# A fused transpose-and-gate product taken apart: plain transposes, column quarters and a summing product in a retention and mixture-of-experts kernel

## The chip, the cores and the metric

The kernel runs on one core of a Trainium2 chip. The metric is the time of one execution on the device in microseconds (us). TensorE is called PE (its weight loads PEld), VectorE DVE, ScalarE ACT, GpSimd POOL, and SyncE SP; SP only issues transfers here.

## The reference

Retention over q, k and v (4 batches, 8 heads, 768 tokens, 64 dims) gives x with 3072 tokens of 512 features. x goes through a noisy top-2 gate over 8 experts and two-layer experts.

```python
gamma = 1.0 - 2.0 ** (-5.0 - np.arange(H))
for t in range(S):
    state = gamma[None, :, None, None] * state + np.einsum('bhd,bhe->bhde', k[:, :, t], v[:, :, t])
    y[:, :, t] = scale * np.einsum('bhd,bhde->bhe', q[:, :, t], state)
x = y.transpose(0, 2, 1, 3).reshape(B * S, H * D)
...
logits = x @ w_gate
noisy_logits = logits + np.log1p(np.exp(x @ w_noise)) * noise
top2 = np.argpartition(-noisy_logits, 2, axis=1)[:, :2]
# top2_w: softmax of the two chosen noisy logits
...
out[mask] += top2_w[mask, k, None] * (np.maximum(x[mask] @ w1[e], 0.0) @ w2[e])
```

## The kernel before, in words

The tokens are cut into 24 tiles of 128 (6 chunks for each of 4 batches). One loop over the tiles, j = 0 to 23, computes the retention, writes x as two f16 halves to xbuf in HBM, and makes the gate logits. Behind it the experts run one after another: `mm1` (L858 to L860, three f16 products for each block) and `mm2` (L890 to L892), with rows gathered from xbuf and added into `out` by indirect transfers.

The order of the work on each engine is the order in which the Python code calls it: the schedule is manual, the engines run their own queues in order, and semaphores join them. `todo`, `mid`, `middle` and `first_todo` are tables from a loop index to extra work (expert 0's weights, the routing of earlier tiles); `at` and `P` enter things in them. After the loop `early(n)` issues the next n units of expert 0's `mm1` between routing steps.

One iteration j does, on PE, in this order: `qk(j+1)` (L327, scores of the next tile, two row halves of the array at once), `x_turn(j-1)` (L375 and L379), `y_state(j)` (L342, four quarters of the array), `y_mm(j)` (L349, two column halves) and the state update pU (L358, column halves; not in the last chunk of a batch, and no `y_state` in the first).

`x_turn` is called the turn below. y lies by feature in four groups of 128. Its f32 products take a group as the weights and multiply it by `turn`, a table of 144 columns: the identity (128) beside 16 columns of gate weights. So one product gives the group by token and its part of the 16 logits; the pairs of groups accumulate in PSUM so that two partial logits are left (`lgs`). L379 sums squares of a token over the features with four one-column products.

On DVE, `qk`'s scores are masked (`am`), then `x_scale(j-1)` makes a power-of-two scale from the sum of squares (p2m, xsa), then come the `mid` entries, then `x_split`'s low half (L405). On ACT: `x_split`'s high half (x), `logits(j-1)` (copy of `lgs`), the copies yt and U, the squares sq, and the `first_todo` entries. POOL scales v (vp) and q (qs). `turn_table` fills the two tables on DVE in iterations 0 and 3, once the constants `ct` (with the identity) and the weights `wgf` have landed. `route_x` adds the two partial logits (lg, L416) and applies softplus on ACT.

SP issues the loads of tile j+4, the x writes (L406), expert 0's weights, `x_t` (a transposing transfer of gathered rows) and the seven writes of zeros into `out` (L273, L276), two of them in iterations 22 and 23.

Of the kernel before, what the change touches and what calls it, by code (L numbers as in the profile page):

```python
# [10 lines left out]
F32 = mybir.dt.float32  # L11
# [5 lines left out]
OP = mybir.AluOpType  # L17
# [3 lines left out]
C = 128  # L21
# [24 lines left out]
XW = 128 + 2 * E  # L46
# [7 lines left out]
for _n, _w in (("mask", 128), ("vtab", NC * H), ("gtab", NC * HP), ("ident", 128), ("tri", 128), ("lanes", 128), ("blks", NCOL),  # L54
               ("lidx", NL), ("base", NL), ("rcap", E - 1), ("tie", E - 1), ("tok1", NCH), ("tokv", NCH * 2), ("pad", 1), ("i64", 64)):
    _C[_n] = (_o, _o + _w)
    _o += _w
CW = _o
SOON = _C["gtab"][1]
# [3 lines left out]
def _constants():  # L63
# [6 lines left out]
    put("ident", np.eye(128))  # L70
    put("mask", p[None, :] >= p[:, None])
# [26 lines left out]
def moe_kernel(ctx, tc, qT, kT, kt, vt, noise, wgn, w1, w2, ctab, qtab, xbuf, out):  # L98
# [21 lines left out]
    ct = consts.tile([128, CW - SOON], F32, name="ct")  # L120

    def K(n):
        a, b = _C[n]
        return cs[:, a:b] if b <= SOON else ct[:, a - SOON:b - SOON]

    wgf = consts.tile([128, 2 * KT * 2 * E], F32, name="wgf")
# [25 lines left out]
    turn = consts.tile([128, 2, KT, XW], F32, name="turn")  # L152
# [125 lines left out]
    def turn_table(v):  # L278

        w = wgf.rearrange("p (v k e) -> p v k e", v=2, e=2 * E)[:, v].rearrange("p (s k) e -> p s k e", s=2)  # L280
        t = turn[:, v].rearrange("p (s k) x -> p s k x", s=2)
        for k in range(2):
            nc.vector.tensor_copy(t[:, :, k, k * 2 * E:k * 2 * E + 128], ident[:, None, :].to_broadcast([128, 2, 128]))
            nc.vector.tensor_copy(t[:, :, k, 128 - k * 128:XW - k * 128], w[:, :, k])

# [5 lines left out]
    VP, AM, QS, PY, PT, YT, XS, SQ, LG = {}, {}, {}, {}, {}, {}, {}, {}, {}  # L291
# [24 lines left out]
    nc.scalar.dma_start(ct, ctab[:, SOON:])  # L316
    q_table(2)
    nc.scalar.dma_start(wgf, wgn)
# [26 lines left out]
    def y_mm(j):  # L345
        c = j % NC
        for i in range(HP):
            for s in range(2):
                nc.tensor.matmul(yplace(j, i, s), VP[j][:, 2 * i + s, :], AM[j][:, s, i, :],  # L349
                                 start=(not c and i < 2), stop=True, skip_group_check=True)  # L350
        YT[j] = loads.tile([128, 2, 2, C], F32, name="yt", bufs=2)
        y = YT[j].rearrange("p s g c -> p (s g c)")
        nc.scalar.activation(y.rearrange("p (s x) -> p s x", s=2), PY.pop(j)[:, :, :2 * C], AF.Copy)
        if c < NC - 1:
            for i in range(HP):
                for s in range(2):
                    h = 2 * i + s
                    nc.tensor.matmul(pU[s * 64:s * 64 + 64, i, :], IN["kt", j][:, h * 64:h * 64 + 64], VP[j][:, h, :],  # L358
                                     start=(c == 0 and i == 0), stop=True, skip_group_check=True)
            nc.scalar.activation(U[(c + 1) % 2], pU, AF.Copy)  # L360
        SQ[j] = loads.tile([128, KT, C], BF, name="sq", bufs=1)
        nc.scalar.activation(SQ[j].rearrange("p n c -> p (n c)"), y, AF.Square)

    def x_turn(j):
# [3 lines left out]
        t = loop_psum.tile([128, 2, 512], F32, name="pT").rearrange("p s x -> p (s x)")  # L368
        PT[j] = p = t[:, 512 - 2 * XW:512 + 2 * XW]
        p = p.rearrange("p (s x) -> p s x", s=2)  # L370
        PT[j, "s"] = t[:, 512 + 2 * XW:513 + 2 * XW]
        y = YT.pop(j)
# [7 lines left out]
        PT[j, "y"] = PT[j].rearrange("p (n x) -> p n x", x=XW)[:, :, :128]  # L380

    def logits(j):
        g = min(j // NC, 3) // 2 + j // (3 * NC)
        c0, n = SPAN[g]
        p = PT.pop(j)
        if j == c0:
            LG[g] = temp([128, n, 2 * E], F32, "lg", n)
            LG[g, "s"] = temp([128, n, 2, 2 * E], F32, "lgs", n)
        nc.scalar.activation(LG[g, "s"][:, j - c0], p.rearrange("p (s x) -> p s x", s=2)[:, :, 128:XW], AF.Copy)
# [7 lines left out]
    def x_split(j, between=None):  # L397
        x = work.tile([128, 2, DM], F16, name="x16", bufs=3)
        py = PT.pop((j, "y"))
        xv = [x[:, a].rearrange("p (n x) -> p n x", n=KT) for a in range(2)]  # L400
# [9 lines left out]
    def route_x(g, c0, c1):  # L410
# [4 lines left out]
        ls = LG[g, "s"][:, c0:c1]  # L415
        nc.vector.tensor_tensor(LG[g][:, c0:c1], ls[:, :, 0], ls[:, :, 1], op=OP.add)  # L416
# [352 lines left out]
    at(21, x_t, 0, 1)  # L769
# [10 lines left out]
    at(0, turn_table, 0)  # L780
    at(3, turn_table, 1)
# [20 lines left out]
    for i in range(2):  # L802
        at(22 + i, zero_out, i)
# [147 lines left out]
    early(1)  # L951
# [9 lines left out]
    early(2)  # L961
# [12 lines left out]
    early(1)  # L974
# [216 lines left out]
```

## Time and profile before

| | us |
|---|---|
| median of 3 runs | 670.21 |
| lowest and highest run | 668.01 and 672.22 |
| the profiled execution | 668.68 |
| its span, first to last instruction | 666.8 |

The profiled execution is one execution of the same program, so a row of it stands against 668.68, of which 1.9 us lie outside the span. Times within the span count from its start. A product's start in PE's timeline is when it is issued; its listed length runs to its result and overlaps the next, so the time that a block takes is read from its start to the start of the next block.

### The profile page before, as it was taken

The page shows a single profiled execution, that of the slowest core. Times are in us where ns is not written, and L with a number is a line of the kernel's source. Part 1 is how long each engine was busy: PE and PEld are TensorE (multiplying, and loading weights), DVE is VectorE, ACT ScalarE, POOL GpSimd, SP SyncE. Part 2 cuts the span into 40 slices and gives each one's busy share as a digit, 9 for nine tenths or more (in the row PEclk, how much of TensorE's full clock was granted, in tenths as well). Part 3 has the DMA queues.
Part 4 walks back from the last instruction along what each step waited for, and adds up shares of the span by engine and source line. Part 5 has one row for each costly group of instructions (what it writes and reads, how often), then busy time and mean ns, then how long its engine had stood idle before and what let it go on. Part 6 is the DMA issues. An engine that isn't in the chain of part 4 may idle for free.

```text
span 666.8 us, 12957 instructions
## 1 busy us (share of the span) xinstructions
PE 644.3 (97%) x5305; PEld 398.9 (60%) x5305; DVE 292.3 (44%) x711; ACT 297.2 (45%) x544; POOL 201.6 (30%) x158
## 2 busy tenths in 40 slices
PE   7999999999999999999999999999999999999991
PEld 5998888648678645554555455545554565455540
DVE  4668887799775221622162216221622162214110
ACT  4678665214544443444454445444444354433210
POOL 3555454042243054104330432043204410440111
PEclk9999999999999999999999999999999999999997
DMA  9999988947297456645673567466736672662212
GB/s 325 394 385 389 342 287 225 364 104 252 73 182 228 119 105 127 196 131 98 124 202 129 97 126 203 124 98 124 205 119 106 122 230 83 126 113 31 32 16 34
DMA packets 90861, 112.87 MB, mean 169 GB/s; under 512 B 57232, under 2 KB 57616, under 8 KB 87216
## 3 DMA queue, kind: packets, MB, share of 16 engines
q1 hardware_dynamic: 78736, 84.95, 41.7%
q0 software_dynamic: 11344, 26.22, 21.2%
q8 instruction: 43, 0.70, 0.4%
q10 hardware_dynamic: 720, 0.84, 0.4%
q14 instruction: 18, 0.15, 0.1%
HBM read 72.67 MB, written 26.21 MB: 148 GB/s over the span
## 4 chain that ended last, share of the span: by engine, by line
PE 74%; DVE 4%; DMA 4%; issue 3%; ACT 1%; POOL 1%; POOLq 0%; ACTq 0%
PE pH L858 12%; PE pH L860 11%; PE pH L859 11%; PE pO L892 11%; PE pO L890 11%; PE pO L891 11%; DMA out<-ot,idx 2%; PE pT L375 1%; DMA xe<-xg 1%; PE pY L349 1%; PE pA L327 1%; PE pT L905 1%; PE pT L904 1%; PE pT L903 1%; DVE w2l L227 1%
## 5 line engine op out<-in xcount | busy, mean ns | idle before, releaser
L879 POOL DMA_INDIRECT out<-ot,idx x54 | 90.7, 1680 | 341.6 <-ACT ot L874 217.2
L858 PE MATMUL pH<-xe,w1h 128*128 128x384 f16 (+5 forms) x576 | 180.9, 314 | 0.9 <-DVE hl L862 0.4
L860 PE MATMUL pH<-xe,w1l 128*128 128x384 f16 (+5 forms) x576 | 181.0, 314 | 0.0
L859 PE MATMUL pH<-xe,w1h 128*128 128x384 f16 (+5 forms) x576 | 181.0, 314 | 0.0
L891 PE MATMUL pO<-w2l,hh 128*128 128x512 f16 x384 | 145.6, 379 | 0.4 <-DVE w2l L227 0.4
L892 PE MATMUL pO<-w2h,hl 128*128 128x512 f16 x384 | 145.6, 379 | 0.1
L890 PE MATMUL pO<-w2h,hh 128*128 128x512 f16 x384 | 145.6, 379 | 0.0
L862 DVE SCALAR_TENSOR_TENSOR hl<-pH,hh 128x384 f16<-128x384 f32 (+5 forms) x144 | 75.1, 526 | 144.9 <-ACT hh L861 144.7
L861 ACT ACTIVATE hh<-pH 128x384 f16<-128x384 f32 (+5 forms) x144 | 67.0, 466 | 132.0 <-PE pH L860 117.7
L874 ACT ACTIVATE ot<-pO,gse 128x512 f32<-128x512 f32 (+4 forms) x54 | 37.1, 687 | 171.7 <-PE pO L892 161.2
L220 DVE SCALAR_TENSOR_TENSOR w1l<-wst,wsc,w1h 128x1024 f16<-128x1024 f32 x28 | 35.8, 1284 | 105.2 <-ACT w1h L215 105.2
L724 POOL DMA_INDIRECT xg<-xbuf,idx x54 | 57.1, 1058 | 64.1 <-DVE wacc L632 31.9
L859 PEld LDWEIGHTS <-w1h 128*128 128x128 f16 x576 | 56.3, 98 | 31.0 <-issue 1.4
L860 PEld LDWEIGHTS <-w1l 128*128 128x128 f16 x576 | 56.2, 98 | 31.0
L858 PEld LDWEIGHTS <-w1h 128*128 128x128 f16 x576 | 56.3, 98 | 30.8 <-issue 0.6
L192 ACT ACTIVATE junk<-wst 128x1024 bf16<-128x1024 f32 x64 | 67.2, 1049 | 0.0
L892 PEld LDWEIGHTS <-hl 128*128 128x128 f16 x384 | 37.5, 98 | 46.6 <-issue 1.0
L890 PEld LDWEIGHTS <-hh 128*128 128x128 f16 x384 | 37.5, 98 | 44.8 <-ACT junk L192 0.3
L891 PEld LDWEIGHTS <-hh 128*128 128x128 f16 x384 | 37.5, 98 | 44.0
L299 POOL TENSOR_TENSOR vp<-in_v,cs 128x512 f32<-128x512 f32 x24 | 26.3, 1094 | 47.2 <-issue 26.9
L215 ACT ACTIVATE w2h<-wst,wsc 128x1024 f16<-128x1024 f32 x32 | 36.5, 1140 | 1.4 <-DVE wsc L170 1.4
L215 ACT ACTIVATE w1h<-wst,wsc 128x1024 f16<-128x1024 f32 x32 | 36.1, 1138 | 1.2 <-DVE wsc L170 1.2
(170 smaller groups left out, 651.0 us busy)
## 6 DMA issues: line engine op xcount, KB each, us to landing
wst<-w SPq DMA_DIRECT2D x28, 1024.0 KB, 7.6
in_q<-qT SPq DMA_DIRECT2D x24, 256.0 KB, 5.8
in_k<-kT SPq DMA_DIRECT2D x24, 256.0 KB, 5.7
in_v<-vt SPq DMA_DIRECT2D x24, 256.0 KB, 5.4
in_kt<-kt SPq DMA_DIRECT2D x24, 256.0 KB, 5.2
xbuf<-x SPq DMA_DIRECT2D x24, 256.0 KB, 4.7
out<-zero SPq DMA_DIRECT2D x6, 1024.0 KB, 7.1
wst<-w SPq DMA_DIRECT2D x8, 512.0 KB, 6.0
```

The lines of the kernel that those rows point to most:

```text
L192: nc.scalar.activation(junk, st[:, i * 1024:(i + 1) * 1024], AF.Square, accum_out=ss[:, i:i + 1])
L215: nc.scalar.activation(hi, st[:, i * 1024:(i + 1) * 1024], AF.Copy, scale=sc[:, 0:1])
L724: nc.gpsimd.indirect_dma_start(out=x[:n], out_offset=None, in_=xbuf[:128 + B0 * S] if e == 0 and t < 3 else xbuf, in_offset=bass.IndirectO ...
L858: nc.tensor.matmul(p[:, :n], whi, xh, start=(k == 0), stop=False)
L859: nc.tensor.matmul(p[:, :n], whi, xl, start=False, stop=False)
L860: nc.tensor.matmul(p[:, :n], wlo, xh, start=False, stop=(k == KT - 1))
L861: nc.scalar.activation(hh[:, f, n0:n1], p[:, :n], AF.Relu)
L862: nc.vector.scalar_tensor_tensor(hl[:, f, n0:n1], p[:, :n], 0.0, hh[:, f, n0:n1], op0=OP.max, op1=OP.subtract)
L879: nc.gpsimd.indirect_dma_start(out=out, out_offset=bass.IndirectOffsetOnAxis(ap=idx[:n, i:i + 1], axis=0), in_=ot[:n], in_offset=None, com ...
L890: nc.tensor.matmul(p, a, WT["2h"][:, f, :], start=(f == 0), stop=False)
L891: nc.tensor.matmul(p, a, WT["2l"][:, f, :], start=False, stop=False)
L892: nc.tensor.matmul(p, c, WT["2h"][:, f, :], start=False, stop=(f == FT - 1))
```

## The change

The turn is taken apart. The four groups of y go through plain transposes against the identity into a PSUM bank of their own (pT). The logits are made by feature: four f32 products with the gate weights as the stationary operand, padded to 32 columns, one for each group, each into its own 32 PSUM partitions (a column quarter of the array) of a second bank (pG). ACT copies the quarters to SBUF (gt), and one f32 product with `pick` (`pick(j-1)`, issued in `y_mm(j)` between y_mm's products and the state update) sums them by token. `logits` then copies 16 columns straight to `lg`, so the tables `turn` and the addition in `route_x` go. The identity and `pick` come in a transfer of their own (`ci`), `wgf` is twice as large, and all seven zero writes stand behind the loop. `x_t(0, 1)` moves from `todo` to `mid`.

```diff
 def _constants():
+    put("pick", np.tile(np.eye(32)[:, :2 * E], (4, 1)))
...
-    nc.scalar.dma_start(ct, ctab[:, SOON:])
+    nc.scalar.dma_start(ci, ctab[:, SOON:THEN])
+    nc.scalar.dma_start(wgf.rearrange("p v k e -> p (v k e)"), wgn)
     q_table(2)
-    nc.scalar.dma_start(wgf, wgn)
+    nc.scalar.dma_start(ct, ctab[:, THEN:])
...
         nc.scalar.activation(y.rearrange("p (s x) -> p s x", s=2), PY.pop(j)[:, :, :2 * C], AF.Copy)
+        if j:
+            pick(j - 1)
         if c < NC - 1:
...
             nc.scalar.activation(U[(c + 1) % 2], pU, AF.Copy)
+        if j:
+            logits(j - 1)
         SQ[j] = loads.tile([128, KT, C], BF, name="sq", bufs=1)
...
-        for s in range(2):
-            for g in range(2):
-                nc.tensor.matmul(p[:, s, g * 128:g * 128 + XW], y[:, s, g, :], turn[:, v, 2 * s + g],
-                                 start=(g == 0), stop=True, skip_group_check=True)
+        for n in range(KT):
+            nc.tensor.transpose(p[:, n * C:(n + 1) * C], y[:, n], ident)
+        for n in range(KT):
+            nc.tensor.matmul(t[n * 32:(n + 1) * 32, :C], wgf[:, v, n], y[:, n], start=True, stop=True, skip_group_check=True)
+        PT[j, "s"] = t[:, C:C + 1]
         q = SQ.pop(j)
         for n in range(KT):
             nc.tensor.matmul(PT[j, "s"], q[:, n], oneb[:, 0:1], start=(n == 0), stop=(n == KT - 1), skip_group_check=True)
+        GT[j] = work.tile([128, C], F32, name="gt", bufs=2)
+        nc.scalar.activation(GT[j], t[:, :C], AF.Copy)
+
+    def pick(j):
+        nc.tensor.matmul(PT[j][:, C + 1:C + 1 + 2 * E], GT.pop(j), K("pick"), start=True, stop=True, skip_group_check=True)
...
-        nc.scalar.activation(LG[g, "s"][:, j - c0], p.rearrange("p (s x) -> p s x", s=2)[:, :, 128:XW], AF.Copy)
+        nc.scalar.activation(LG[g][:, j - c0], PT.pop(j)[:, C + 1:C + 1 + 2 * E], AF.Copy)
...
         nc.scalar.activation(xv[0], py, AF.Copy, scale=XS[j])
-        logits(j)
-        if between:
-            between()
...
-        nc.vector.tensor_tensor(LG[g][:, c0:c1], ls[:, :, 0], ls[:, :, 1], op=OP.add)
...
-    at(21, x_t, 0, 1)
+    P(21, x_t, 0, 1)
...
-    at(0, turn_table, 0)
-    at(3, turn_table, 1)
...
-    for i in range(2):
-        at(22 + i, zero_out, i)
...
     early(1)
-    zero_out(2)
+    zero_out(0)
+    zero_out(1)
     x_turn(j)
     x_scale(j)
-    x_split(j, lambda: route_x(2, 0, NC))
+    x_split(j)
+    early(1)
+    pick(j)
+    logits(j)
+    route_x(2, 0, NC)
     route_d(1)
...
-    early(1)
+    zero_out(2)
     zero_out(3)
...
-    early(2)
+    early(3)
...
-    early(1)
     own_c(1)
```

On PE, one iteration of the loop before, from the last sum of squares of one tile to the first of the next:

```order
L379 MATMUL pT<-oneb,sq 128x1
L342 MATMUL pY<-qs,U_160 64x128 x8
L349 MATMUL pY<-am,vp 64x128 x8
L358 MATMUL pU<-vp,in_kt 64x64 x8
L327 MATMUL pA<-qs,in_k 128x128 x8
L375 MATMUL pT<-turn,yt 128x144 x4
L379 LDWEIGHTS sq
```

and the same iteration after:

```order
L377 MATMUL pG<-oneb,sq 128x1
L337 MATMUL pY<-qs,U_160 64x128 x8
L344 MATMUL pY<-am,vp 64x128 x8
L382 MATMUL pG<-ci,gt 128x16
L355 MATMUL pU<-vp,in_kt 64x64 x8
L322 MATMUL pA<-qs,in_k 128x128 x8
L371 MATMUL pT<-ci,yt 128x128 x4
L373 MATMUL pG<-yt,wgf 32x128 x4
L377 LDWEIGHTS sq
```

The summing product (L382) stands between y_mm and pU, and the turn is two blocks (L371, L373) in place of one.

On ACT, where expert 0's first weights are cast (w1h) ahead of the turn's readers, before (with what each instruction waits for):

```order
L362 ACTIVATE sq<-yt 128x512 [waits Activation_49]
L215 ACTIVATE w1h<-wst_391,wsc_393 128x1024 [waits DVE_49]
L215 ACTIVATE w1h<-wst_391,wsc_393 128x1024
L401 ACTIVATE x_1007<-pT,xsa 128x512 [waits DMAHW0_49,DVE_49,PE_49]
L389 ACTIVATE lgs_310<-pT 128x32
L353 ACTIVATE yt<-pY 128x512 [waits PE_49]
```

and after:

```order
L361 ACTIVATE sq<-yt 128x512 [waits Activation_49]
L217 ACTIVATE w1h<-wst_401,wsc_403 128x1024 [waits DVE_49]
L217 ACTIVATE w1h<-wst_401,wsc_403 128x1024
L379 ACTIVATE gt<-pG 128x128 [waits PE_49]
L401 ACTIVATE x_1077<-pT,xsa 128x512 [waits DMAHW1_49,DVE_49]
L348 ACTIVATE yt<-pY 128x512 [waits PE_49]
```

The copy gt comes in ahead of x, behind the casts, and the copy of the logits has left this place.

On DVE, the same place in the loop, x_scale and what stands behind it, before:

```order
L330 TENSOR_TENSOR am<-pA,cs 128x512 [waits PE_49] x2
L394 TENSOR_SCALAR p2m<-pT 128x1 [waits PE_49]
L395 TENSOR_SCALAR xsa<-p2m 128x1 [waits DVE_49]
L227 SCALAR_TENSOR_TENSOR w1l<-wst_391,wsc_393,w1h 128x512 [waits Activation_49]
L227 SCALAR_TENSOR_TENSOR w1l<-wst_391,wsc_393,w1h 128x512
L227 SCALAR_TENSOR_TENSOR w1l<-wst_391,wsc_393,w1h 128x512 [waits Activation_49]
L405 SCALAR_TENSOR_TENSOR x_1007<-pT,xsa,x_1007 128x512 [waits DMAHW0_49,DVE_49,Activation_49]
```

and after:

```order
L325 TENSOR_TENSOR am<-pA,cs 128x512 [waits PE_49] x2
L394 TENSOR_SCALAR p2m<-pG 128x1 [waits Activation_49]
L395 TENSOR_SCALAR xsa<-p2m 128x1 [waits DVE_49]
L229 SCALAR_TENSOR_TENSOR w1l<-wst_401,wsc_403,w1h 128x512 x3
L402 SCALAR_TENSOR_TENSOR x_1077<-pT,xsa,x_1077 128x512 [waits DMAHW1_49,Activation_49]
```

p2m waited for PE and now waits for ACT; the instruction that it waits for is gt.

## Rows read from the trace of the kernel before

**Rows 1.** The page: the span, and part 1, busy time of each engine.

```profile
span 666.8 us, 12957 instructions
PE 644.3 (97%) x5305; PEld 398.9 (60%) x5305; DVE 292.3 (44%) x711; ACT 297.2 (45%) x544; POOL 201.6 (30%) x158
```

**Rows 2.** The table by stretch: us; busy time and count of PE, PEld, DVE, ACT, POOL; PEclk; DMA; GB/s.

```profile
20.00:117.00 97.00, 93.72 (x1556) 84.04 (x1547) 74.21 (x245) 64.47 (x138) 49.43 (x43) 1.00 0.97 336
200.00:640.00 440.00, 439.87 (x2844) 242.30 (x2843) 137.09 (x240) 189.71 (x313) 117.27 (x87) 1.00 0.56 129
```

**Rows 3.** Waits of PE and its weight loads, 0 to 130 us: total, times, longest.

```profile
PEld pT L375 <- ACT sq L362: 3.0, 6, 1.1
PEld pT L375 <- issue: 1.1, 1, 1.1
PEld pT L375 <- ACT yt L353: 0.4, 1, 0.4
PEld pT L375 <- ACT U L360: 0.2, 1, 0.2
PEld pA L327 <- POOL qs L305: 1.3, 1, 1.3
PE pA L327 <- DVE turn L284: 1.2, 1, 1.2
```

**Rows 4.** PE's timeline, turn of tile 20 to 21: start, us, engine, line, tile, array cut.

```profile
102.78 1.16 PE L327 MATMUL pA<-qs,in_k 64*128 64x128 f32 x16
103.87 1.25 PE L375 MATMUL pT<-turn,yt 128*128 128x144 f32 x8
104.96 0.24 PE L379 MATMUL pT<-oneb,sq 128*128 128x1 bf16 x4
105.13 0.67 PE L342 MATMUL pY<-qs,U 64*64 64x128 f32 x16
105.73 1.09 PE L349 MATMUL pY<-am,vp 128*64 128x128 f32 x16
106.65 0.63 PE L358 MATMUL pU<-vp,in_kt 128*64 128x64 f32 x16
107.22 1.16 PE L327 MATMUL pA<-qs,in_k 64*128 64x128 f32 x16
108.31 1.25 PE L375 MATMUL pT<-turn,yt 128*128 128x144 f32 x8
```

**Rows 5.** PE's timeline, four transposes between mm1 products.

```profile
194.20 0.60 PE L914 MATMUL pO<-ct,yt 128*64 128x128 f32 x4
194.64 0.27 PE L858 MATMUL pH<-xe,w1h 128*128 128x256 f16 x1
```

**Rows 6.** The timeline of weight loads where L202 stands between L358 and L327.

```profile
51.62 0.10 PEld L202 LDWEIGHTS <-oneb 128*128 128x128 bf16 x1
51.73 0.64 PEld L327 LDWEIGHTS pA<-qs,in_k 64*128 64x128 f32 x10
```

**Rows 7.** ACT's timeline, a copy of 32 columns and one of 256.

```profile
101.82 0.19 ACT L389 ACTIVATE lgs<-pT 128x32 f32<-128x32 f32 x1
102.94 0.38 ACT L360 ACTIVATE U<-pU 128x256 f32<-128x256 f32 x1
```

**Rows 8.** ACT's timeline, iteration 10.

```profile
53.26 2.19 ACT L215 ACTIVATE w1h<-wst,wsc 128x1024 f16<-128x1024 f32 x2
```

**Rows 9.** DVE's timeline, iteration 10.

```profile
54.40 0.15 DVE L394 TENSOR_SCALAR p2m<-pT 128x1 int32<-128x1 int32 x1
...
56.64 0.74 DVE L405 SCALAR_TENSOR_TENSOR x<-pT,xsa,x 128x512 f16<-128x512 f32 x1
```

**Rows 10.** DVE's timeline, iteration 18: the lg addition.

```profile
94.32 0.44 DVE L416 TENSOR_TENSOR lg<-lgs 128x96 f32<-128x96 f32 x1
```

**Rows 11.** The chain that ended last: start, us, what.

```profile
153.74 10.86 DMA out<-ot,idx
```

**Rows 12.** SP's timeline: two transposes of xg in one row.

```profile
107.71 3.52 SPq L731 DMA_TRANSPOSE xe<-xg  x2
```

More of the change, by code (lines that the diff above doesn't have):

```diff
@@ L53 @@
 _o = 0
-for _n, _w in (("mask", 128), ("vtab", NC * H), ("gtab", NC * HP), ("ident", 128), ("tri", 128), ("lanes", 128), ("blks", NCOL),
+for _n, _w in (("mask", 128), ("vtab", NC * H), ("gtab", NC * HP), ("ident", 128), ("pick", 2 * E), ("tri", 128), ("lanes", 128), ("blks", NCOL),
                ("lidx", NL), ("base", NL), ("rcap", E - 1), ("tie", E - 1), ("tok1", NCH), ("tokv", NCH * 2), ("pad", 1), ("i64", 64)):
@@ L58 @@
 CW = _o
-SOON = _C["gtab"][1]
+SOON, THEN = _C["gtab"][1], _C["pick"][1]
 WARM, BUSY = 10, 4
@@ L119, in moe_kernel @@
     cs = consts.tile([128, SOON], F32, name="cs")
-    ct = consts.tile([128, CW - SOON], F32, name="ct")
+    ci = consts.tile([128, THEN - SOON], F32, name="ci")
+    ct = consts.tile([128, CW - THEN], F32, name="ct")
     def K(n):
         a, b = _C[n]
-        return cs[:, a:b] if b <= SOON else ct[:, a - SOON:b - SOON]
-    wgf = consts.tile([128, 2 * KT * 2 * E], F32, name="wgf")
+        if b <= SOON:
+            return cs[:, a:b]
+        return ci[:, a - SOON:b - SOON] if b <= THEN else ct[:, a - THEN:b - THEN]
+    wgf = consts.tile([128, 2, KT, 32], F32, name="wgf")
     nz = consts.tile([128, NCH, E], F32, name="nz")
@@ L151, in moe_kernel @@
     xsa = consts.tile([128, NCH], F32, name="xsa")
-    turn = consts.tile([128, 2, KT, XW], F32, name="turn")
     pR = psum.tile([128, 512], F32, name="pR")
@@ L276, in zero_out @@
             nc.sync.dma_start(out[:128, :], zero)
[L278 to L284, printed above, removed]
     U = []
@@ L367, in x_turn @@
         v = int(b >= B0)
[L368 to L372, printed above, removed]
-        for s in range(2):
-            for g in range(2):
-                nc.tensor.matmul(p[:, s, g * 128:g * 128 + XW], y[:, s, g, :], turn[:, v, 2 * s + g],
-                                 start=(g == 0), stop=True, skip_group_check=True)
+        PT[j, "y"] = p = loop_psum.tile([128, 512], F32, name="pT")
+        PT[j] = t = loop_psum.tile([128, 512], F32, name="pG")
+        y = YT.pop(j).rearrange("p s g c -> p (s g) c")
+        for n in range(KT):
[3 more added lines that the diff above has]
+        PT[j, "s"] = t[:, C:C + 1]
         q = SQ.pop(j)
@@ L395, in x_scale, with x_split @@
         nc.vector.tensor_scalar(XS[j].bitcast(I32), m[:, :1], -1.0, float((127 + TX + 62) << 23), op0=OP.mult, op1=OP.add)
-    def x_split(j, between=None):
+    def x_split(j):
         x = work.tile([128, 2, DM], F16, name="x16", bufs=3)
         py = PT.pop((j, "y"))
-        xv = [x[:, a].rearrange("p (n x) -> p n x", n=KT) for a in range(2)]
+        xv = [x[:, a] for a in range(2)]
         nc.scalar.activation(xv[0], py, AF.Copy, scale=XS[j])
-        logits(j)
-        if between:
-            between()
         nc.vector.scalar_tensor_tensor(xv[1], py, XS[j], xv[0], op0=OP.mult, op1=OP.subtract)
@@ L807, in moe_kernel @@
     qk(0)
-    t = loop_psum.tile([128, 2, 512], F32, name="pT")
+    t = loop_psum.tile([128, 512], F32, name="pT")
     for i in range(BUSY):
-        nc.tensor.matmul(t[:, 0], warm[:, :128], warm, start=True, stop=True)
+        nc.tensor.matmul(t, warm[:, :128], warm, start=True, stop=True)
     for j in range(NCH):
@@ L1172 @@
     nz[:, B0 * NC:] = nz[:, B0 * NC:][:, :, turn]
-    wg = [np.concatenate([moe_w_gate[:, o], moe_w_noise[:, o]], 1)[PERM].reshape(KT, 128, 2 * E).transpose(1, 0, 2)
+    wg = [np.pad(np.concatenate([moe_w_gate[:, o], moe_w_noise[:, o]], 1)[PERM], ((0, 0), (0, 32 - 2 * E)))
+          .reshape(KT, 128, 32).transpose(1, 0, 2)
           for o in (list(range(E)), turn)]
```

9 lines of the change are left out of this document (2 added, 7 removed).

## The prediction

> **What bounds the kernel now.** I read the page first. TensorE (PE) is busy for 644.3 of 666.8 us [rows 1], so I asked where its idle time lies. The table of stretches says: in the token loop (20 to 117 us) PE is busy for 93.7 of 97 us at a granted clock of 1.00, and from 200 to 640 us for 439.9 of 440 [rows 2]. Nothing behind the loop can soak up a delay, so what the loop gains or loses arrives at the end almost one for one.
>
> Inside the loop I read PE's own timeline from turn to turn (L375 of tile 20 at 103.87 to L375 of tile 21 at 108.31, 4.44 us) [rows 4], and count iterations that way below, by the tile whose turn ends them. PE goes from block to block without idle time, so only the cost of the blocks counts. Last I read what the turn itself, the block that is rewritten, waits for: its weight loads waited 4.7 us in all, in nine of the iterations [rows 3]. The loop has that slack and no more.
>
> **What a change of tile shape costs now.** The blocks of [rows 4] use different cuts of the array: L327 two row halves, L375 and L379 the whole, L342 four quarters, L349 and L358 two column halves. A lone f32 pass of 128 columns takes 0.11 us: the four transposes of L914 take 194.20 to 194.64 [rows 5]. L349 has 16 passes, two abreast: 8 x 0.11 = 0.88 of its 0.92. L342 has 16, four abreast: 4 x 0.11 = 0.44, but lasts 0.60. L327 has 16, two abreast: 0.88, but lasts 1.09. L358, 64 columns wide, should take 8 x 0.055 = 0.44 and lasts 0.57. L349 is followed by a block of its own shape; the other three are followed by another shape and carry 0.16, 0.21 and 0.13 us more than their passes. So a change of shape costs 0.13 to 0.21 us, and the changed loop has more of them.
>
> **The change, part by part.**
>
> *The turn on PE.* Now: L375 with 8 passes of 144 columns, 1.09 us, and L379, 0.17: 1.26 us. Then: four transposes, one pass each (L914 shows one each), 0.44, and a change to column quarters behind them, for which I take 0.20, like L327, which also loads 128 columns of f32: 0.64. Then eight passes of 128 columns for the logits, four abreast, as L342 runs them: 2 x 0.11 + 0.16 = 0.38. Then L379's four, 0.17. Together 1.19 us: only 0.07 less than now. If the changes of shape were free it would be 0.44 + 0.22 + 0.17 = 0.83.
>
> *The product that sums the quarters* stands between L349 and L358, which run today with no change of shape between them. It is f32, whole array, so two passes with two weight loads and 16 columns each, too short to hide a load. The nearest row is L202, one product of 4 columns between L358 and L327, where a change exists anyway: 0.11 us from 51.62 to 51.73 [rows 6]. So the lower bound is 0.11; with a change in (0.16), twice 0.11, and a change out (0.13) it is 0.50. I take 0.50, because both changes are new. In iterations without L358 (5 and 23; the last chunk of a batch keeps no state) one change is there already: 0.34.
>
> PE's iteration thus grows by 0.50 - 0.07 = 0.43 us, by 0.27 in iterations 5 and 23. [...]
>
> *A longer chain from PE to DVE.* x_scale's first step on DVE (p2m) waited for PE's squares; it now waits for ACT's copy gt, as the order shows. gt has 128 columns; the copies of 32 and of 256 take 0.19 and 0.38 us [rows 7], so I take 0.25, and with the extra handover 0.27. The product waits for p2m too, but stands 1.5 us of PE work (L342, L349) behind the turn [rows 4], so that costs nothing by itself. The logits copy moves on ACT from ahead of yt to just ahead of the squares, which PE needs only after the transposes and the quarters, a microsecond into the turn: nothing. Where the turn waits for x_split (iterations 9 to 12, 15, 17 to 19), this lies on the path. Iteration 10 is worse: ACT runs two w1h casts from 53.26 for 2.19 us [rows 8]. p2m ran at 54.40, beside them; gt stands behind them in ACT's queue and ends at about 55.7, so p2m, the three w1l steps queued behind it on DVE, the low half of x (56.64) [rows 9] and the next turn move by 1.3 us. The other seven I put at 0.26 on average: 0.27 for gt or, where PE becomes the later one, 0.43 less the old wait, less the lg addition (0.44 us) [rows 10], which leaves DVE's chain in two of them.
>
> *DVE's turn tables* go. The 1.2 us that PE waited for them ahead of L327 is not won: the same L327 also waited for POOL's qs (1.3 us) [rows 3], which nothing moves. *The small transfers* on ACT's queue are one more, with some 64 KB more of weights; against 0.97 of DMA share in the loop [rows 2] I count nothing, at most half a microsecond either way.
>
> *Zero writes and x_t on SP's queue.* Two writes of 1 MB leave iterations 22 and 23 and are issued behind the loop with the other five; one transpose goes ahead of tile 20's x write. Behind them on SP stand the x writes of the last tiles and, much later, the next weight loads. The scatter into out ran at 153.74 [rows 11], 37 us behind the loop's end, so writes that come some 2 us later are hidden; without that cover it would cost those 2 us. The transposes, issued by 111.2 [rows 12], have a longer loop to land in.
>
> *Behind the loop* the mm1 units change places by one, and as many of them stand ahead of the last routing steps as before. One lg addition leaves DVE's chain (-0.44) and with it a handover from ACT; gt (0.27) comes in, and PE gets the last product between whole-array matmuls, where no shape changes (twice 0.11), beside DVE's chain: -0.3 us, at most 0.3 the other way.
>
> **The sum.** Iterations bound by PE: 12 x 0.43 = 5.2; iterations 5 and 23: 0.5; iteration 22, where PE waits 0.4 for yt [rows 3] and the product fills that wait: 0.15. The eight that wait: 1.3 + 7 x 0.26 = 3.1. Loop +9.0, behind it -0.3: **+8.7 us**. The profiled execution took 668.68 us, so 677.4; the median of the runs is 1.5 higher, 670.21, which makes **679 us**.
>
> **Rivals.**
>
> 1. *The turn gets cheaper, and the kernel is not slower* (chance 0.19). If the added loads and changes of shape overlap with the passes as L202's nearly does, an iteration has 0.44 + 0.22 + 0.17 + 0.11 = 0.94 in place of 1.26. It decides when the 0.74 us that I add for loads and changes is really under 0.32. Fully so, 15 iterations give -4.8, the eight about +1: 666 us. For it: L349's passes show almost no extra. Against it: L342, L327 and L358 each carry theirs, in the same places of every iteration. [...]
>
> 2. *The quarters run one after another* (0.10). Then their eight passes take 0.88, not 0.22: +0.66 in each of 15 iterations, and gt and p2m come later by as much in the eight: about 14 more, 693 us. Against it: L342 has four tiles at once. For it: those differ in rows too, which the four quarters do not.
>
> 3. *The gt chain decides in more iterations* (0.10): with 0.8 in four more places where ACT's queue holds a cast or a sum ahead of gt, +3: 682 us.
>
> 4. *The zero writes meet the weight loads or the scatter* (0.03): 681 us.
>
> 5. *The clock falls* (0.01). [...]
>
> **How the numbers follow.** The forecast has 0.57 and by itself spans 672 to 684: the change of shape between 0.13 and 0.21, the product between 0.2 and 0.6. To 8 in 10 I reach down to 668, which takes in about half of rival 1, and up to 689; rivals 2 and 5 and the rest of rival 1 stay out. A difference under 1% (6.7 us) is about what runs of this kernel can't tell from none. Above 676.9: 0.35 of the forecast and 0.24 of rivals 2 to 5: 0.59. Within: 0.22 of the forecast and 0.15 of rival 1: 0.37. Under 663.5: 0.04, for a rival 1 that gains on DVE's side too.
>
> **What would show it.** In the changed loop's timeline L371 to L373 about 0.64, L373 to L377 about 0.38, L382 to L355 about 0.5 apart, and an undisturbed iteration near 4.87 us; p2m idle before it until gt; the first L858 near 124 us in place of 115, and from there on the same lengths as now. I am wrong if L382 lies within 0.2 us, or if the quarters' eight passes start one behind another.

## The result and the profile after

The changed kernel is slower: a median of 678.6 us (676.24 to 680.84, six runs) against 671.96 us for the kernel before in the same six rounds (668.01 to 673.9), a ratio of 1.0118 with a 95% interval of 1.0088 to 1.0149. The profiled execution took 676.53 us (668.68 before); the sum had said 677.4 for it and 679 for the median.

The page, its span and busy times, and the table by stretch (columns as in [rows 2]):

```profile
span 674.7 us, 13272 instructions
...
PE 652.3 (97%) x5449; PEld 395.2 (59%) x5449; DVE 292.5 (43%) x699; ACT 304.0 (45%) x568; POOL 201.5 (30%) x158
```

```profile
20.00:117.00 97.00, 92.30 (x1551) 74.14 (x1543) 70.35 (x219) 66.89 (x151) 50.15 (x43) 1.00 0.93 322
...
200.00:640.00 440.00, 439.75 (x2887) 245.13 (x2883) 141.97 (x259) 191.67 (x316) 119.64 (x89) 1.00 0.57 132
```

Behind the loop PE is as full as before [rows 2]. The loop ends later, as PE's timelines show, first that of the kernel before:

```profile
115.12 0.34 PE L858 MATMUL pH<-xe,w1h 128*128 128x384 f16 x1
```

```profile
123.65 0.32 PE L849 MATMUL pH<-xe,w1h 128*128 128x384 f16 x1
```

The first mm1 product starts 8.5 us later. In what follows "the loop's end" is the start of that product. From there to the first mm2 product (L890 before, L881 after) it is 17.76 us before and 17.49 after, so 0.27 came back behind the loop. The span grew by 7.9, but what is left of the difference can't be put down to the change: from the loop's end to the end of the span the traces of all versions take 551.1 to 555.8 us, and the changed kernel and sums_apart, which have the same work there, differ by 1.8.

PE's timeline from the turn of tile 20 to that of 21, to be read against [rows 4]:

```profile
106.93 0.65 PE L371 MATMUL pT<-ci,yt 128*128 128x128 f32 x4
107.52 0.42 PE L373 MATMUL pG<-yt,wgf 128*32 128x128 f32 x8
107.88 0.25 PE L377 MATMUL pG<-oneb,sq 128*128 128x1 bf16 x4
108.06 0.67 PE L337 MATMUL pY<-qs,U 64*64 64x128 f32 x16
108.66 1.09 PE L344 MATMUL pY<-am,vp 128*64 128x128 f32 x16
109.68 0.40 PE L382 MATMUL pG<-ci,gt 128*128 128x16 f32 x2
110.01 0.69 PE L355 MATMUL pU<-vp,in_kt 128*64 128x64 f32 x16
110.62 1.16 PE L322 MATMUL pA<-qs,in_k 64*128 64x128 f32 x16
111.71 0.66 PE L371 MATMUL pT<-ci,yt 128*128 128x128 f32 x4
```

From start to start: the transposes take 0.59, the quarters 0.36, the sums 0.18, a turn of 1.13 us in place of 1.26. The product has 0.33 of its own, and the blocks around it have grown, L344 from 0.92 to 1.02 and L355 from 0.57 to 0.61: 0.47 in all. The iteration is 4.78 in place of 4.44, 0.34 longer.

That is not the whole. Taken turn by turn against the kernel before, the loop's 8.5 us are: 4.4 in the twelve iterations that PE bounds, 0.3 in iterations 5 and 23, 0.2 in 22, and 3.85 in the eight that wait (9 to 12, 15, 17 to 19), less 0.25 of a first turn that came earlier. The eight are very uneven: iteration 10 grew by 1.70, 11 by 0.97 and 17 by 1.09, while 15 shrank by 0.64. The table of waits, 0 to 135 us, has three of them (10, 11 and 17) as one long wait of the turn each; the kernel before had four such waits of 1.9 us in all:

```profile
PE pT L371 <- DVE x L402: 4.5, 3, 1.8
```

What DVE does there shows why. DVE's timeline in iteration 10, then POOL's, then DVE's in iterations 15 and 17:

```profile
58.04 0.16 DVE L394 TENSOR_SCALAR p2m<-pG 128x1 int32<-128x1 int32 x1 [0.96 <-ACT gt L379]
58.23 0.15 DVE L395 TENSOR_SCALAR xsa<-p2m 128x1 int32<-128x1 int32 x1
58.30 2.88 DVE L229 SCALAR_TENSOR_TENSOR w1l<-wst,wsc,w1h 128x512 f16<-128x512 f32 x3
61.11 0.74 DVE L402 SCALAR_TENSOR_TENSOR x<-pT,xsa,x 128x512 f16<-128x512 f32 x1
```

```profile
59.60 1.04 POOL L293 TENSOR_TENSOR vp<-in_v,cs 128x512 f32<-128x512 f32 x1 [2.61 <-issue]
60.60 1.71 POOL L299 TENSOR_TENSOR qs<-in_q,gq 128x512 f32<-128x512 f32 x1
```

```profile
85.30 0.27 DVE L492 TENSOR_TENSOR gateb<-t 128x108 f32<-128x108 f32 x1
...
94.47 0.96 DVE L530 CAST tokb<-gr 128x12 bf16<-128x12 f32 x1
95.47 1.20 DVE L531 TENSOR_TENSOR tokb<-gr,tokb 128x12 bf16<-128x12 f32 x1
```

And in the kernel before, DVE in iterations 10, 15 and 17:

```profile
54.65 2.07 DVE L227 SCALAR_TENSOR_TENSOR w1l<-wst,wsc,w1h 128x512 f16<-128x512 f32 x3
...
79.08 1.14 DVE L497 TENSOR_TENSOR gateb<-t 128x108 f32<-128x108 f32 x1
...
88.34 0.19 DVE L535 CAST tokb<-gr 128x12 bf16<-128x12 f32 x1
```

p2m waits 0.96 for gt: such a wait was forecast. But the three w1l steps behind it take 2.88 us in place of 2.07, with the same shapes, and POOL's qs beside them takes 1.71 in place of the usual 1.27. In the kernel before they were done at 56.7, and POOL began vp at 56.46. Taken one by one (shortest, median and longest in ns, then the first and the last start), two of the three are as short as before, and the last one, which starts at 59.6 like vp, is twice as long:

```profile
L229 DVE SCALAR_TENSOR_TENSOR w1l<-wst,wsc,w1h x3: 744/745/1561, 58.3 to 59.6; 128x512 f16<-128x512 f32 x3
```

In iteration 17 a cast of 12 columns takes 0.96 in place of 0.19; in iteration 15 it is the other way round, gateb's 1.14 of before is 0.27 now. Each long one starts just behind the start of a vp or a qs of POOL and is not done before that one is: the cast runs from 94.47 to 95.43, vp from 94.35 to 95.39. I call this a collision; the prediction had none. In iteration 10 the start of w1l, counted from its turn, moved by 0.89 and its length by 0.81; in iteration 11 by 0.18 and 0.78. So of the 3.85 us 1.6 are collisions, net (0.81 + 0.78 + 0.91 of iteration 17 - 0.87 of iteration 15). The 2.2 that are left were not measured by themselves: they hold the longer chain to DVE and, where PE ends last, its longer blocks.

### The profile page after: what moved, and what is told of

The parts are those of the page before. It is cut to its first block, busy times and chain, and to the rows that moved or that the text cites. A ratio compares the mean times of both kernels' runs of the same rounds, so it can differ in the third digit from the quotient of the medians.

```text
span 674.7 us, 13272 instructions
## 1 busy us (share of the span) xinstructions
PE 652.3 (97%) x5449; PEld 395.2 (59%) x5449; DVE 292.5 (43%) x699; ACT 304.0 (45%) x568; POOL 201.5 (30%) x158
## 4 chain that ended last, share of the span: by engine, by line
PE 82%; DVE 10%; DMA 4%; ACT 2%; issue 1%; POOL 0%; SPq 0%; POOLq 0%; ACTq 0%
PE pH L849 11%; PE pH L850 11%; PE pH L851 11%; PE pO L881 11%; PE pO L883 11%; PE pO L882 11%; PE pY L344 3%; PE pA L322 2%; DMA in_k<-kT 2%; PE pT L371 2%; PE pU L355 1%; PE pY L337 1%; DVE bb L606 1%; PE pG L373 1%; DVE hl L853 1%; DVE w1l L229 1%
## 5 line engine op out<-in xcount | busy, mean ns | idle before, releaser
L870 POOL DMA_INDIRECT out<-ot,idx x54 | 88.8, 1644 | 343.2 <-ACT ot L865 213.6
L881 PE MATMUL pO<-w2h,hh 128*128 128x512 f16 x384 | 145.5, 379 | 0.0
L719 POOL DMA_INDIRECT xg<-xbuf,idx x54 | 59.2, 1096 | 62.1 <-DVE wacc L627 31.8
L881 PEld LDWEIGHTS <-hh 128*128 128x128 f16 x384 | 37.5, 98 | 44.8 <-ACT junk L194 0.3
L325 DVE TENSOR_TENSOR am<-pA,cs 128x512 f32<-128x512 f32 x48 | 30.8, 683 | 14.7 <-PE pA L322 14.4
```

The source lines that it names most:

```text
L719: nc.gpsimd.indirect_dma_start(out=x[:n], out_offset=None, in_=xbuf[:128 + B0 * S] if e == 0 and t < 3 else xbuf, in_offset=bass.IndirectO ...
L870: nc.gpsimd.indirect_dma_start(out=out, out_offset=bass.IndirectOffsetOnAxis(ap=idx[:n, i:i + 1], axis=0), in_=ot[:n], in_offset=None, com ...
L881: nc.tensor.matmul(p, a, WT["2h"][:, f, :], start=(f == 0), stop=False)
```

## The experiments

The theory after the first reading has three parts: a price for changes of tile shape on PE, p2m's wait for gt, and DVE steps that slide beside POOL's. The rivals stand in the expectations. Ratios are to the kernel before, run beside each version on the same chip. Beside late_apart, squares_first, by_token, before_product and twelve_places the kernel before took 675 us, 5 us more than beside the others, and no trace of it was taken there; verdicts on a few us therefore go by the traces' own loops, and the ratios stand beside them.

### The sums of squares in another bank (sums_apart)

gt (ACT) and p2m (DVE) read different columns of one PSUM bank, and their order was kept by a wait (0.96 us in iteration 10). With the sums elsewhere p2m waits for PE again, and in iteration 10 it starts right behind am (56.82).

```diff
-        PT[j, "s"] = t[:, C:C + 1]
+        PT[j, "s"] = pR[:, 496:497]
```

> The sums of squares go to a column of another PSUM bank than the quarters, so that x_scale's first step p2m waits for PE again and not for ACT's copy gt; everything else is the changed kernel. Theory: the loop's growth of 8.5 us is 0.34 us of PE blocks in each iteration that PE bounds, about 2.2 us of p2m's wait for gt in the eight that wait for x_split, and about 1.6 us net of DVE steps that have slid beside POOL's work (the w1l steps of iterations 10 and 11 take 0.95 us each in place of 0.69). Then iteration 10 falls from 6.30 to 4.7 to 5.0 us, w1l is back at 0.69 there, and the first mm1 product moves from 123.65 to between 120.3 and 121.5. Rival A, the turn waits for x_split because of ACT's casts whatever p2m waits for: first mm1 within 0.4 of 123.65. Rival B, w1l is slow for a reason other than where it falls: iteration 10 near 5.4, w1l still 0.95.

672.43 us, ratio 1.0031 (1.0005 to 1.0057). The loop's end is at 119.57, 4.1 us earlier than in the changed kernel and 0.7 earlier than the range that I gave. DVE's timeline of this kernel:

```profile
57.07 2.07 DVE L229 SCALAR_TENSOR_TENSOR w1l<-wst,wsc,w1h 128x512 f16<-128x512 f32 x3
...
61.85 2.07 DVE L229 SCALAR_TENSOR_TENSOR w1l<-wst,wsc,w1h 128x512 f16<-128x512 f32 x3
```

w1l is back at 2.07 in both iterations, with the same casts ahead of it on ACT. (The expectation's 0.95 for each step was the mean of three, of which one was long.) Iteration 10 is 4.79, 11 is 4.43, and the eight iterations together are level with the kernel before (-0.04 in place of +3.85). An undisturbed iteration stays at 4.78. So the wait for gt, with the collisions that it led to, cost 3.9 us: 1.51 in iteration 10, 1.01 in 11, 1.22 in 17 and 0.17 in 18. Iterations 9, 12, 15 and 19 are as in the changed kernel. So what they gained or lost is not gt's: 9 and 19 grew by a quarter of a us, and 15 gained its 0.64, without that wait too. Rivals A and B fall.

### POOL held back (pool_behind)

```diff
+        late = j in (10, 11, 17)
+        if j + 1 < NCH and not late:
             v_scale(j + 1)
...
         for f, a in mid.get(j, []):
             f(*a)
+        if late:
+            v_scale(j + 1)
+            q_scale(j + 2)
...
+            nc.vector.memset(VP[j][:, 0, 0:1], 0.0)
```

> In iterations 10, 11 and 17 POOL's vp waits until DVE's steps ahead of x_split's low half are done (a one-column DVE write into vp's tile, which vp then overwrites), so that vp and qs no longer run beside them; gt and the product stay as changed. Theory of collisions: the three w1l steps of iteration 10 take 2.07 us in place of 2.88, those of 11 too, the cast tokb of 17 takes 0.19 in place of 0.96; the first mm1 product comes 1.8 to 2.6 us earlier, near 121.5. Rival, these steps are slow through ACT's casts or the transfers: same durations, first mm1 at 123.6 or, if the late vp holds PE up, later.

686.7 us, ratio 1.0241 (1.0175 to 1.0308), the loop's end at 134.74: the durations came as the theory said, the time did not. DVE's and PE's timelines, and the table by stretch:

```profile
57.52 2.06 DVE L229 SCALAR_TENSOR_TENSOR w1l<-wst,wsc,w1h 128x512 f16<-128x512 f32 x3
```

```profile
62.05 2.08 PE L324 MATMUL pA<-qs,in_k 64*128 64x128 f32 x16 [3.39 <-POOL qs L301]
```

```profile
62.00:64.00 2.00, 1.95 (x16) 1.78 (x16) 0.00 (x0) 0.00 (x0) 0.00 (x1) 0.50 0.43 136
```

With POOL quiet w1l takes 2.06 even behind the same wait for gt, and the cast of iteration 17 takes 0.19; that shows the collision by itself. But qs is needed at the start of the next iteration, which I had overlooked, so PE waited 9.4 us in three places. The second thing to see is the granted clock: 0.50 from 62 to 64, right behind a wait of 3.39 us, and L324's block takes 2.01 in place of 1.09.

### A slide put into the kernel before (before_slide)

```diff
+    first_todo[9].insert(1, (lambda: nc.scalar.activation(junk, ST["1", 0][0][:, :1024], AF.Square), ()))
```

> The kernel before with one step more on ACT (a square of 128x1024 into a junk tile, about 1.05 us) ahead of the two casts of iteration 10, so that DVE's w1l steps slide by about 1 us against POOL's vp, as they did behind gt; PE is not touched. Theory of collisions: the three w1l steps take 2.5 to 3.0 us in place of 2.07, iteration 10 grows by 1.5 to 2.0 us, more than the 1.05 put in. Rival, a step's length doesn't depend on where it falls: 2.07, and iteration 10 grows by 1.05 or less. The time of the whole kernel can't tell (under 0.3%); the trace does.

670.72 us, ratio 1.001 (0.9984 to 1.0035). DVE's and POOL's timelines:

```profile
55.09 2.86 DVE L227 SCALAR_TENSOR_TENSOR w1l<-wst,wsc,w1h 128x512 f16<-128x512 f32 x3 [0.56 <-ACT w1h L215]
```

```profile
56.25 1.15 POOL L299 TENSOR_TENSOR vp<-in_v,cs 128x512 f32<-128x512 f32 x1 [2.34 <-issue]
57.36 1.72 POOL L305 TENSOR_TENSOR qs<-in_q,gq 128x512 f32<-128x512 f32 x1
```

A slide of 0.65 us of w1l against its turn made iteration 10 longer by 1.44, the other 0.79 being w1l's own length; no other iteration moved by more than 0.01. The growth is a little under the forecast 1.5, but more than the 1.05 put in. So it is the place beside POOL that makes the step long, not anything of the changed turn. Again it is the last of the three, at 1.53, and the other two take 0.74 and 0.75.

Both timelines agree: the one long w1l step starts just behind vp's start and ends behind vp's end (56.42 to 57.95, vp 56.25 to 57.40), qs grows by 0.44 (1.28 to 1.72), and am, whose source is PSUM, kept its mean of 0.68. What makes the step wait there is not shown.

### The product twice, and alone (pick_twice, before_product)

```diff
-        nc.tensor.matmul(PT[j][:, C + 1:C + 1 + 2 * E], GT.pop(j), K("pick"), ...)
+        g = GT.pop(j)
+        for i in range(2):
+            nc.tensor.matmul(PT[j][:, C + 1:C + 1 + 2 * E], g, K("pick"), ...)
```

> The summing product is issued twice in a row with the same operands and result. Theory: its 0.43 us are two short passes of 0.11 and two changes of tile shape; the second product stands between whole-array neighbours and adds 0.20 to 0.24 us, an undisturbed iteration is 4.98 to 5.02 us, the first mm1 product near 127. Rival, shape changes cost nothing and the product's passes with their weight loads cost it all: 0.40 or more each, an iteration 5.18 or more, first mm1 at 130.

682.3 us, ratio 1.0175 (1.0119 to 1.0231). PE's timeline and the table by stretch:

```profile
111.33 0.62 PE L384 MATMUL pG<-ci,gt 128*128 128x16 f32 x4
111.88 0.69 PE L355 MATMUL pU<-vp,in_kt 128*64 128x64 f32 x16
```

```profile
100.00:108.00 8.00, 8.00 (x72) 6.57 (x70) 3.81 (x9) 3.95 (x9) 2.27 (x2) 0.50 0.81 269
```

Two products take 0.55, one took 0.33: the second costs 0.22, an iteration is 5.00. So of the 0.47, 0.22 are the product and 0.25 the two changes of shape. The loop's end, 131.20, is not the forecast 127: in iterations 18 and 19 the granted clock was 0.50, behind a wait of 1.62 us for x_split, and they took 4.1 us more than 0.22 each explains. Without that the end would be at 127.1. That this meets the forecast is partly luck, since iteration 10 is 1.00 shorter than in the changed kernel: its w1l steps had all begun when vp began (61.81) and took 2.07. The rival's 0.40 for each product falls.

The kernel before with such a product alone, from the identity, between L349 and L358:

```diff
+        if j:
+            nc.tensor.matmul(pR[:, 490:506], ident, ident[:, :16], start=True, stop=True, skip_group_check=True)
         if c < NC - 1:
```

> The kernel before with one thing added: in every iteration from 1 on, a product like the summing one (f32, whole array, 16 columns, from the identity, result not used) between L349 and L358. Theory: 0.43 us in each iteration that PE bounds, half of it the two changes of shape: an undisturbed iteration of 4.85 to 4.89 us, the first mm1 product between 120.5 and 123 since the waiting iterations absorb some, ratio 1.007 to 1.011. Rival, the price came with the changed turn (waits for gt, the bank it writes): 4.66 and 117 to 118.5.

677.95 us, ratio 1.0044 (1.0011 to 1.0077), below the range that I gave; the loop's end is inside it. PE's timeline:

```profile
112.30 1.09 PE L349 MATMUL pY<-am,vp 128*64 128x128 f32 x16
113.32 0.39 PE L355 MATMUL pR<-ct 128*128 128x16 f32 x2
113.64 0.57 PE L360 MATMUL pU<-vp,in_kt 128*64 128x64 f32 x12
```

L349 takes 1.02 and the product 0.32, as in the changed kernel, an undisturbed iteration is 4.91, 0.47 more than before and a little over the 4.89 that I gave, and the loop ends at 122.56, 7.4 us later. A product in this place alone costs nearly what the whole change costs in the loop; the eight iterations that wait take up some of it.

### The product elsewhere (pick_late, late_apart, squares_first)

```diff
+        if j > 1:
+            pick(j - 2)
+            logits(j - 2)
         if j:
             x_turn(j - 1)
```

> The summing product of a tile stands one iteration later, between the scores of L322 and the transposes of the next turn, where a change to the whole array exists anyway; its result goes to spare columns of pU's bank, and the copy of the logits and the softplus come right behind it. Theory: the product costs 0.20 to 0.25 in place of 0.43, an undisturbed iteration 4.55 to 4.60 us in place of 4.78, the first mm1 product near 120.5, the time 1.006 to 1.008 of the kernel before. Rival, the price is the product's own: 4.78 and 123.6.

674.76 us, ratio 1.0067 (1.0039 to 1.0095). This kernel changes part of the computation: its product starts anew in the bank in which pU is summed, and its output is off by a relative 0.58; that the state is not carried on is my reading of this and was not shown. PE's blocks are the same. Its timeline:

```profile
111.12 0.40 PE L379 MATMUL pU<-ci,gt 128*128 128x16 f32 x2
111.36 0.64 PE L368 MATMUL pT<-ci,yt 128*128 128x128 f32 x4
```

The product costs 0.24, as forecast, and the iteration is 4.52, just under the 4.55 that I gave as the least. The ratio lies in the range, but the loop's end, 122.91, is not 120.5: against the kernel before iterations 10, 11 and 18 lost 5.5 us. p2m still waits for gt, which now also stands behind the copy of the logits, and w1l takes 3.86 beside vp and qs in iteration 10. The clock fell behind waits of 2.66 us (granted 0.57 from 63 to 67) and 1.84 us (0.76 from 95 to 100).

With the sums apart, and the product's result beside y in pY's banks:

```diff
+        nc.tensor.matmul(PY[i][:, 0, 2 * C:2 * C + 2 * E], GT.pop(j), K("pick"), start=True, stop=True, ...)
```

> The changed kernel with both mends: the sums of squares in a bank of their own, and the summing product one iteration later, ahead of the transposes of the next turn, its result in spare columns of pY's banks (of the tile that is written next). Theory: an undisturbed iteration is 4.52 us, as the product cost 0.24 there, and no iteration waits for gt; the first mm1 product lies between 114.5 and 116.5 us, level with the kernel before (115.12), and the time within 0.4% of it. Rival, the later product brings waits of its own: ACT's copy of the logits holds gt up, iterations 10 and 17 are over 5.5 us, first mm1 near 119.

674.85 us, ratio 0.9998 (0.9965 to 1.0031), but the loop's end is at 121.72. So the theory fails and the rival is nearer: iteration 10 is 7.73, though 17, which the rival had over 5.5, is 4.74. PE's waits and ACT's timeline:

```profile
PE pY L336 <- ACT lg L384: 2.6, 3, 1.5
```

```profile
54.71 2.19 ACT L217 ACTIVATE w1h<-wst,wsc 128x1024 f16<-128x1024 f32 x2
56.81 0.16 ACT L384 ACTIVATE lg<-pY 128x16 f32<-128x16 f32 x1
```

The undisturbed iteration is 4.52 again, but y's products wait for the copy of the logits out of the same bank, and that stands behind two casts. Behind the longest of these waits, 1.53 us, the clock fell (granted 0.89 from 54 to 70, 1.00 on both sides), and L343's block takes 1.76 in place of 0.92; that and the blocks beside it are 1.6 of iteration 10's 7.73.

With the sums ahead of the quarters as well:

```diff
+        q = SQ.pop(j)
+        for n in range(KT):
+            nc.tensor.matmul(PT[j, "s"], q[:, n], oneb[:, 0:1], ...)
         for n in range(KT):
             nc.tensor.matmul(t[n * 32:(n + 1) * 32, :C], wgf[:, v, n], y[:, n], ...)
```

> As the run with both mends, and the sums of squares stand ahead of the column quarters, so that product, transposes and sums are one block of whole-array tiles and the quarters are followed by L337's array quarters. Theory, every change of shape costs 0.13 to 0.21 us: one change fewer, an undisturbed iteration of 4.31 to 4.39 us, less than the 4.44 of the kernel before, the first mm1 product 1 to 3 us earlier than with both mends. Rival, the price belongs to the quarters' block and not to the change: 4.52 and no gain.

674.56 us, ratio 0.9989 (0.9958 to 1.0021). An iteration is 4.42, from one row of transposes to the next:

```profile
22.13 0.64 PE L366 MATMUL pT<-ci,yt 128*128 128x128 f32 x4
...
26.55 0.64 PE L366 MATMUL pT<-ci,yt 128*128 128x128 f32 x4
```

One change of shape fewer is worth 0.10, less than the 0.13 that I gave as the least. The loop's end is at 120.46; the waits for the copy are the same or longer, and the clock fell here too (0.89 from 54 to 70).

### Logits by token (by_token)

```diff
-            nc.tensor.matmul(t[n * 32:(n + 1) * 32, :C], wgf[:, v, n], y[:, n], start=True, stop=True, ...)
+            nc.tensor.matmul(t[:, :2 * E], y[:, n], wgf[:, v, n, :2 * E], start=(n == 0), stop=(n == KT - 1), ...)
```

> Of the changed turn the plain transposes alone: the logits come by token from four products with y as weights and 16 columns of gate weights, all whole-array, accumulated in one place; no quarters, no gt, no summing product. Theory: each such product costs what the second of the pair cost, 0.22 us, so the turn has 0.44 + 0.88 + 0.17 = 1.49 in place of 1.26 and an undisturbed iteration 4.65 to 4.70 us; p2m waits for PE, so the other eight lose little: first mm1 product at 118 to 119.5 us, ratio to the kernel before 1.003 to 1.007. Rival, the transposes against the identity are themselves dearer than in the fused product: iteration over 4.8.

676.34 us, ratio 1.0027 (0.9999 to 1.0055). PE's timeline:

```profile
111.72 0.66 PE L369 MATMUL pT<-ci,yt 128*128 128x128 f32 x4
112.22 0.96 PE L371 MATMUL pG<-wgf,yt 128*128 128x16 f32 x8
113.03 0.24 PE L375 MATMUL pG<-oneb,sq 128*128 128x1 bf16 x4
113.20 0.67 PE L337 MATMUL pY<-qs,U 64*64 64x128 f32 x16
```

The turn is 1.48, an iteration 4.65, the loop's end 118.97, all as forecast; the ratio is just under its range. Plain transposes with four short products lose 3.9 us in the loop, less than half of what the changed kernel loses; most of that difference is the wait for gt, since with the sums apart the quarters and the product lose 4.4. The eight passes of 16 columns take 0.81 here, 0.10 each, nearly the 0.11 of a pass of 128 columns [rows 5]: the fused product of the kernel before carries its 16 columns along with the 128 and has no such passes.

### The small parts alone (before_small)

```diff
-    at(21, x_t, 0, 1)
+    P(21, x_t, 0, 1)
...
-    for i in range(2):
-        at(22 + i, zero_out, i)
...
     early(1)
+    zero_out(0)
+    zero_out(1)
     zero_out(2)
```

> The kernel before with the small parts of the change alone: all seven zero writes behind the loop, and the second transpose of tile 20's rows in the earlier place. Theory: nothing that the measurement can tell, ratio 0.998 to 1.002, first mm1 product within 0.5 us of 115.12, the scatter into out not held up. Rival, the writes collide with the weight loads behind the loop: 2 us later, 1.003.

670.44 us, ratio 1.0015 (0.999 to 1.004), the loop's end at 114.88: nothing that can be told. The interval alone would not shut out the rival's 1.003, but the trace shows the scatters into out on time: the first starts at 145.50, and at 145.75 in the kernel before. The first turn came 0.24 earlier here too, and 0.20 earlier in before_slide and before_product, which change nothing ahead of it, so that part of the changed kernel's loop is not the missing turn tables.

### The version that the runs point to (spare_columns, twelve_places)

```diff
+    pLG = pUL[:, 256:256 + 2 * NC * 2 * E].rearrange("p (c e) -> p c e", c=2 * NC)
...
+        nc.tensor.matmul(pLG[:, j % NC + NC * (j >= 3 * NC)], GT.pop(j), K("pick"), start=False, stop=True, ...)
...
+        nc.scalar.activation(LG[g][:, c0:c1], pLG[:, NC * (g == 2):NC * (g == 2) + NC], AF.Copy)
```

> As squares_first, but the summing product's result goes to spare columns of pU's bank, a place of its own for each of six tiles, and one copy takes six tiles to the logits, so that no product of y waits for ACT's copy of the logits. Theory: that wait, behind ACT's casts, was what the later product brought in (10 us over the loop); an undisturbed iteration stays at 4.42 us, and the waiting iterations are like those of the kernel before: first mm1 product between 113 and 116 us, time within 0.5% of the kernel before, not clearly faster. Rival, the waits come from the later product itself (gt is held up by casts and the product by gt): iteration 10 still over 7 us, first mm1 at 119 or more.

> As spare_columns, with places of their own for the last six tiles too: there the last tile's product was added onto that of tile 17, since no state update starts anew in between, so one tile of 24 was routed by the wrong logits. Theory: the loop's end doesn't hang on that: an undisturbed iteration of 4.42 us, first mm1 product between 112.3 and 113 us, time 0.993 to 0.997 of the kernel before, faster than both kernels. Rival, the gain came from the last tile's other routing: ratio 0.998 or more with the same end of the loop.

spare_columns, in which the logits of the last tile hold those of tile 17 as well: 666.05 us, ratio 0.9949 (0.9931 to 0.9966), the loop's end at 112.59. twelve_places, where each has its own place: 672.57 us beside 675.18 of the kernel before, ratio 0.9953 (0.9925 to 0.9981), the loop's end at 114.28, later than forecast. All of PE's waits in twelve_places from 20 to 125 us:

```profile
PE pU L380 <- ACT U L357: 1.5, 2, 1.0
PE pT L369 <- DVE s L206: 0.6, 1, 0.6
PE pT L369 <- DVE x L399: 0.2, 1, 0.2
```

An undisturbed iteration is 4.42 in both, iteration 10 is 4.42 and iteration 17 is 3.95 (4.60 and 4.98 before). In twelve_places the product of iteration 20 waited 1.0 for ACT's copy of U out of the same bank, which is most of the 1.7 between the two ends. So the changed turn need not be slower: the loop ends ahead of that of both kernels if the product stands beside whole-array work, nothing waits for its copy, and p2m doesn't wait for gt. The time is half a per cent under the kernel before, but of these 3 us the loop of twelve_places explains 0.8, and 0.3 of that is a first turn that came earlier; where the rest comes from is not shown.

## Why the prediction was right, and where it was not

The time, 679, was met at 678.6, and its loop of +9.0 at +8.5 (first mm1 product at 123.65 for 124). That it came so near is partly luck. Two terms were off in opposite directions, and the 679 was built on a median of 670.21, while the kernel before took 671.96 beside the changed one: for the forecast 8.7 the medians differ by 6.6 and the profiled executions by 7.85.

*PE's blocks, 0.43 in an iteration: right in kind, too large.* The product has 0.47 for the forecast 0.50; its passes, twice 0.11, are shown by the second product, and its two changes of shape cost 0.25, not 0.16 + 0.13. L382 to L355 is 0.33, not the 0.5 named as a sign, since the rest shows in the blocks beside it. The turn gained 0.13, not 0.07: the change from the transposes to the quarters came at 0.15, where I took 0.20. Twelve times 0.34 to 0.50 make 4.4 for the forecast 5.2, and iterations 5 and 23 have 0.3 for 0.5. The large one of the twelve, iteration 3 at 0.50, holds a collision of its own. DVE's timeline there, just behind the starts of POOL's vp (22.30) and qs (23.30):

```profile
22.35 1.08 DVE L825 CAST trib<-ct 128x128 bf16<-128x128 f32 x1
23.35 1.31 DVE L825 CAST lanes<-ct 128x128 bf16<-128x128 f32 x1
```

These casts stand ahead of am in the chain that ended last; in the kernel before they take 0.22 each. They do so in by_token too, where the small transfers come in the changed order, so the transfers, which I had counted at nothing, are not the cause.

*The eight that wait, 3.1: the step that failed.* It said that in iteration 10 DVE's work moves by 1.3 and in the other seven by 0.26. In iteration 10 the chain moved 0.89: ACT's two casts began 0.33 behind the turn in the kernel before and 0.03 ahead of it in the changed one, so gt stood less far behind. Of the other seven, sums_apart shows a cost of gt in 11, 17 and 18 alone. What made up for this is that a moved step meets other neighbours: 0.81, 0.78 and 0.91 of collisions in iterations 10, 11 and 17, a term that the sum did not have. I had read what p2m would wait for, but not what would run beside w1l after it had moved. sums_apart, pool_behind and before_slide show this from three sides. The 4.7 us of slack that I had counted were those of the weight loads alone; PE itself had waited 1.9 us more there for x_split.

*Behind the loop, -0.3:* -0.27 up to the first mm2 product. The same stretch is 17.76 to 17.77 in before_small, before_slide and before_product and 17.50 in sums_apart and pool_behind, so that is the change's own.

*Rivals.* That changes of shape come free fell with pick_twice and before_product. That the quarters run one after another fell with 0.36 for eight passes. Of four more places at 0.8 for the gt chain two came, 11 and 17, grown by 0.97 and 1.09, but mostly through collisions. The zero writes are hidden, as before_small shows; the scatter at 153.74 that I had set them against is the second, and the first, at 145.75, is not held up either. The 0.01 for a fallen clock rests on no run: none shows a loop at a lower clock throughout. It stayed at 1.00 in the changed kernel's loop (20 to 117 us), with transposes in each iteration; it fell in five of the experiments (pool_behind, pick_twice, pick_late, late_apart and squares_first), each time within 2 us of the end of a wait of PE of 1.53 us or more.

What stays open: why the kernel before took 5 us more beside some versions than beside others, while the edited ones lose less there. It is not the chip alone, since on chip 10 it took 670.57 beside sums_apart and 675.18 beside twelve_places. No trace of the longer runs was taken, and the ratios beside them lie 0.3% to 1.0% under what the loops' ends say.

## What to carry to other kernels

On an engine that is full, count a new short product with the shapes on both sides of it: here the same product cost 0.47 us between two column-half blocks and 0.24 beside whole-array work. When a change moves a step, look at what the step will then run beside, not only at what it waits for: 0.65 us of delay became 1.44. Two engines that read different columns of one PSUM bank may be put in order by a wait, as gt and p2m were here; a column in another bank took 4.1 us off the loop.

## What the runs showed of the hardware that was not expected

A DVE step that starts just behind the start of a vp or a qs of POOL can last until that one is done: one of three w1l steps took 1.53 (before_slide) and 1.56 (the changed kernel) in place of 0.74, the 12-column cast of iteration 17 0.96 in place of 0.19. PE's granted clock fell behind waits of 1.53 us (late_apart, 0.89 from 54 to 70) to 3.39 us (pool_behind, 0.50 from 62 to 64, where a block of 1.09 took 2.01). It does not fall behind each such wait: behind one of 1.84 us it stayed at 1.00 in the changed kernel (97.45) and fell in pick_late (96.41).
